# Last sums of weight conversions moved to GpSimd, two conversions moved out of the prologue, and the split middle products issued last

## The chip, the cores and the metric

The kernel runs on one core of a Trainium2 chip. The metric is device time in microseconds (us) of one execution. The names of the engines are those of the profile: PE is TensorE (matmuls; PEld its weight loads), DVE VectorE, ACT ScalarE, POOL GpSimd, SP the engine that here only issues DMAs. An engine works through its own instructions in the order in which they were issued; engines wait for each other by semaphores. DMAs are issued from the queues of SP, ACT and POOL.

## The reference

Two stages, one behind the other. First a global filter along the sequence: for each of 8 batches and 256 channels, a real Fourier transform over 3008 positions, a product with a complex filter, and the inverse transform. Then a feed-forward layer over all 24064 tokens.

```python
X = np.fft.rfft(x, axis=1)                    # x: (8, 3008, 256)
y = np.fft.irfft(X * (filt_r + 1j * filt_i)[None], n=3008, axis=1)
h = y.reshape(24064, 256) @ w_in              # (256, 2048)
out = (h - np.tanh(h)) @ w_out                # (2048, 256)
```

w_in and w_out come as 64-bit floats, the rest as 32-bit floats. All matmuls are in f32; a matmul stands in the trace as two records, one for each pass over the data.

## The kernel before

**The transform** is written with 3008 = 64 x 47, as matmuls with constant matrices, in three stages per batch. The *first* stage (`first`, product `pf`, line 294 for batches 1 and 2, 306 for the others) takes the 64-point part, four rows per step; its PSUM result is copied by ACT into the tile `a1` (line 296), of which there is one, and written to DRAM. The *middle* stage (`middle`, for batches 1 to 7) takes the 47-point part, the filter and the way back, in four steps `o` per batch. Each step has two matrix products, there and back, through `packed`: 24x24 matrices on 16 tiles of the PE array (four row groups `q`, four column groups `col`), each with 512 columns of data. In the last step, o=3, four of the 16 tiles hold special frequencies: there the 512 columns are split in two matmuls of 256 columns, one with the plain and one with the special matrix (line 358; all others are line 354). The *last* stage (`last`, product `pu`, line 534) gives the token block for the feed-forward layer.

**The feed-forward layer** runs in 48 groups (batch, part), each in four quarters `u` of the 2048 columns: 192 blocks, numbered U. One pass of the loop over U issues the up product of block U, the activation (`shrink`, on ACT lines 687 to 693, then DVE line 697) of block U-1 and the down product of block U-2. For the first group (U=0 to 3) these are plain products (`up_plain`, matmuls line 645, results copied by ACT or DVE in line 648; `down_plain`, line 800). From U=4 on they use a 2x2 block scheme with seven instead of eight products (`up`, line 575, `down`, line 745), for which sums of weight parts (`sums`, lines 223 and 226) and of data (`combine`, lines 555 to 558) are needed. `combine` runs on DVE while weights are still pending, and on POOL afterwards.

**The weights** are converted on the chip. `parts_of` cuts them into 16 jobs, here j0 to j15: j0 and j1 are quarter 0 of w_in (tile `wu`), j2 and j3 quarter 1, j4 and j5 quarter 2, j6 and j7 quarter 0 of w_out (tile `wd`), j8 and j9 quarter 3 of w_in, j10 to j15 the other quarters of w_out. A job is a generator, `converted`: a DMA of 512 KB into a raw buffer (line 169), a step on ACT (line 175), five on DVE (lines 177, 180, 183, 186 and 188) and a final sum of two halves into `wu` or `wd` (line 195; one instruction of 512 columns for w_in, two of 256 for w_out). The generator `weights` goes through a list of jobs, one step for each call of `next`. It issues the load of the job three further on when a job has been issued whole, and starts the next job's ACT step ahead of the current one's line 183. It also puts the calls of `sums(u)` behind certain jobs.

**Order of the work.** All of it is issued in the order of the Python program. The prologue (to line 1209) does batch 0's transform; its loop over seven slots `g` issues, for each, PE products (`across`, `there0`, `back0`), the filter (`filtered`, DVE lines 386 to 398, and on POOL the sum of line 395 for g below 5), and a few steps of the first five conversions (`convert`). At g=1 a row block `neg` is negated and written to `less`, and read back into the filter (line 489, on POOL's queue). At g=2 the raw loads of j5 and j6 are issued on POOL (line 1195). After the prologue's loop `convert(100)` issues what is left of j3 and j4; then come matmuls without use that keep PE busy (`warmer`), and the loop over U.

In the loop, the callbacks d, e, s and t that `up` and `up_plain` call set the order: d and e advance the down product, s the activation, e and the five calls t(0) to t(4) also advance the conversions (`converting`), t issues first-stage steps at the positions `due` (position 5u+k in the first group), middle-stage steps, and copies of the filter in DRAM (`filters_d`, lines 1250 and 1254, on POOL's queue). Four conversion steps are issued ahead of the loop, 14 in each of U=0 and 1, and 22 in each later block, until j15 and the sums of u=0 to 6 are done (103 steps, early in U=5).

In U=0, ACT copies all four up results to SBUF, in order; from U=1 on it copies the first and the third, DVE the second and the fourth.

Of the kernel before, what the change touches and what calls it, by code (L numbers as in the profile page):

```python
# [17 lines left out]
BATCH, SEQ, DM = 8, 3008, 256  # L18
# [9 lines left out]
NX = NH // XH  # L28
# [10 lines left out]
LEAD = 34  # L39
# [72 lines left out]
def kernel(  # L112
# [9 lines left out]
    nc = tc.nc  # L122
    V, G, ACT = nc.vector, nc.gpsimd, nc.scalar
# [41 lines left out]
    def converted(tiles, src, dsts, queue):  # L165

        n = src.shape[-1] * (src.shape[1] if len(src.shape) == 3 else 1)
        t = tiles("raw", I64, n)
        queue.dma_start(t if len(src.shape) == 2 else
                        t.rearrange("p (h n) -> p h n", h=src.shape[1]), src)  # L170
        yield
        words = t.bitcast(I32).rearrange("p (n w) -> p n w", w=2)
        lo, hi = words[:, :, 0].bitcast(U32), words[:, :, 1]
        top, low = tiles("top", I32, n), tiles("low", I32, n)
        ACT.activation(top.bitcast(F32), hi.bitcast(F32), AF.Copy, scale=2.0 ** -112)
        yield
        V.tensor_scalar(out=top.bitcast(F32), in0=top.bitcast(F32), scalar1=-MOST, scalar2=MOST,
                        op0=ALU.max, op1=ALU.min)
        yield
        V.tensor_scalar(out=top, in0=top, scalar1=5, scalar2=2,  # L180
                        op0=ALU.logical_shift_left, op1=ALU.logical_shift_right)
        yield
        V.scalar_tensor_tensor(out=top, in0=hi, scalar=-2 ** 30, in1=top,
                               op0=ALU.bitwise_and, op1=ALU.bitwise_or)
        yield
        V.tensor_scalar(out=low, in0=top, scalar1=-2 ** 23, scalar2=None, op0=ALU.bitwise_and)
        yield
        V.scalar_tensor_tensor(out=low.bitcast(F32), in0=lo, scalar=2.0 ** -52,
                               in1=low.bitcast(F32), op0=ALU.mult, op1=ALU.mult)
        for cols, dst in dsts:  # L190
            yield
            f, p = (v.bitcast(F32)[:, cols] for v in (top, low))
            if len(dst.shape) == 3:
                f, p = (v.rearrange("p (h n) -> p h n", h=dst.shape[1]) for v in (f, p))
            V.tensor_add(dst, f, p)
        yield

    def parts_of(quarters):
# [21 lines left out]
    def sums(u):  # L220

        w = (wu if u < 4 else wd)[:, :, 256 * (u % 4):256 * (u % 4) + 256]
        V.tensor_add(w[:, 4], w[:, 6], w[:, 3])
        yield
        for to, one_in, less in ((5, 4, 0), (2, 1, 5), (6, 0, 6)):
            V.tensor_sub(w[:, to], w[:, one_in], w[:, less])
            yield

    def begun(tiles, job, queue=nc.sync):
        j = converted(tiles, *job, queue)  # L230
        next(j)
        return j
# [112 lines left out]

    def packed(banks, o, weight, data):

        for q, bank in enumerate(banks):
            part = slice(PAD * q, PAD * q + NH)
            for col in range(4):  # L350
                to, at = bank[PAD * col:PAD * col + PAD], data(q, col)[part]
                plain, special = (wide[part, weight(q, col, last)] for last in (0, 1))
                if o < 3 or 3 != (col if weight is WAYS[0] else q):
                    nc.tensor.matmul(to.rearrange("p n c -> p (n c)"), plain, at,  # L354
                                     start=True, stop=True)
                    continue
                for n, way in enumerate((plain, special)):
                    nc.tensor.matmul(to[:, n], way, at[:, n * DM:n * DM + DM],  # L358
                                     start=True, stop=True)

    def forth(g, at, z):

# [584 lines left out]
    with tc.tile_pool(name="tr", bufs=2) as tr, tc.manual_schedule():  # L947
# [16 lines left out]
        with tc.tile_pool(name="pro", bufs=1) as pro, \  # L964
# [106 lines left out]
            jobs = parts_of((0, 1, 2, 4, 3, 5, 6, 7))  # L1071
# [38 lines left out]
            began.append(begun(tiles0, jobs[2], queue=G))  # L1110
            G.dma_start(mats[:, 3 * KM:6 * KM], mats_d[:, 3 * KM:6 * KM])
            fts[1] = filters_of(1)
            began += [begun(tiles0, job, queue=G) for job in jobs[3:5]]
            G.dma_start(mats[0:KH, 6 * KM:], mats_d[0:KH, 6 * KM:])
            turning = turned_rows(tr.tile([128, 2, DM], F32, tag="e1", bufs=2, name="neg")[0:NH, 0])
            next(turning)

            early = weights(tiles0, jobs[:5], G, began, 5)
            next(early)

            def convert(n):
# [44 lines left out]
            for g in range(last_g + 1):  # L1166
# [25 lines left out]
                if g == 1:  # L1192
                    next(turning)
                if g == 2:
                    ahead = [begun(tiles1, job, queue=G) for job in jobs[5:7]]
            rest(0, SG * (last_g - 1), [nc.sync])
            way_back()
            rest(SG * (last_g - 1), NA - SG * (last_g - 1), [nc.sync])
# [2 lines left out]
            fs = first(2, z2, [(1, c) for c in range(2, NX)])  # L1201
            next(fs)
            convert(100)
            late = weights(tiles1, jobs[5:], G, ahead, 3,
                           after={6: (0,), 8: (1,), 10: (2, 3, 4, 5, 6)})
            next(late)
            for _ in ones_1:
                pass
# [2 lines left out]
        with tc.tile_pool(name="dn", bufs=2) as dn, \  # L1211
# [60 lines left out]
                                 start=True, stop=True)  # L1272
            for _ in range(4):
                next(late)
            due = [4 + (LEAD - 4) * k / (NX + 4) for k in range(NX + 4)]
            plan = []
            kinds = {(2, 0): "there", (1, 3): "back"}
            kinds.update({at: "filter" for at in FILTERED})
# [2 lines left out]
            for U in range(total + 2):  # L1281
# [25 lines left out]
                def converting(n):  # L1307

                    for _ in range(n):
                        if next(late, pending) is pending:  # L1310
                            pending.clear()
# [5 lines left out]
                def e():  # L1317

                    next(dw, None)
                    converting(3 if U > 1 else 1)  # L1320

                def s():

# [85 lines left out]
```

## Time and profile before

| | us |
|---|---|
| median of 3 runs | 2591.28 |
| lowest and highest run | 2586.17, 2592.92 |
| profiled execution | 2591.19 |
| its span, first to last instruction | 2589.4 |
| PE busy in the span | 2561.4 |
| granted clock, mean | 0.998 |

The profile has one row for each group of instructions, and a timeline with one row for each run of like instructions: start, duration, engine, line, operation, written tile <- read tiles, shapes and count. In brackets stands how long the engine had been idle before it and what ended the wait. Of an engine's 99% nothing follows for one stretch: the prologue, the first blocks and the long steady part are read one by one. Times in the timeline count from the span's start; the first up product of the loop starts at 88.18 us.

### The profile page before, as it was taken

To read this page: it belongs to the slowest core of one execution; us is meant where nothing else is said; L and a number is where in the kernel's file an instruction comes from. 1 tells how busy PE (TensorE), PEld (TensorE's weight loads), DVE (VectorE), ACT (ScalarE), POOL (GpSimd) and SP (SyncE) were. 2 spreads that over 40 slices of the span, in tenths; PEclk is the share of its full clock that TensorE was granted. 3 is DMA by queue.
4 is the path that set the end of the run, shared out by engine and by line. 5 is a ranking of instruction groups with operands and counts; after the bars stand their busy time and mean duration, and the time that the engine had idled before them with its cause. 6 is when DMAs were issued, how large, how long until landed. Compare 5 with 4: busy or idle time off the path is not lost.

```text
span 2589.4 us, 43444 instructions
## 1 busy us (share of the span) xinstructions
PE 2561.4 (99%) x16596; PEld 2180.3 (84%) x16596; DVE 1818.5 (70%) x2234; ACT 1662.5 (64%) x2482; POOL 1466.0 (57%) x1126
## 2 busy tenths in 40 slices
PE   8999999999999999999999999999999999999998
PEld 6668888888898888988888888888889888898887
DVE  6788776877567775778657876588766877555555
ACT  4566666666666666666666666666666666666665
POOL 4356665665556655665646565466655766545552
PEclk9999999999999999999999999999999999999999
DMA  7873215441433324333243432444231321110110
GB/s 219 259 194 103 64 33 120 110 102 44 95 80 100 89 56 92 84 90 92 49 101 80 101 79 50 94 96 104 65 68 45 93 66 41 35 33 18 25 22 18
DMA packets 345334, 214.32 MB, mean 83 GB/s; under 512 B 245337, under 2 KB 316535, under 8 KB 341469
## 3 DMA queue, kind: packets, MB, share of 16 engines
q1 hardware_dynamic: 321551, 170.82, 28.7%
q10 hardware_dynamic: 12142, 23.60, 3.0%
q0 software_dynamic: 11424, 17.03, 2.4%
q8 instruction: 133, 2.18, 0.4%
q14 instruction: 84, 0.69, 0.1%
HBM read 130.72 MB, written 83.39 MB: 83 GB/s over the span
## 4 chain that ended last, share of the span: by engine, by line
PE 95%; DMA 2%; DVE 1%; ACT 1%; issue 1%; POOL 0%; ACTq 0%; DVEq 0%; POOLq 0%
PE o L745 43%; PE x L575 25%; PE z L575 12%; PE y L575 6%; PE pm L354 2%; PE pu L534 2%; DMA ct<-a 2%; PE pf L306 1%; PE pm L358 1%; PE warm L996 0%; PE pf L986 0%; DMA neg<-in_filt_i_dram 0%; PE o L800 0%; PE pe L1047 0%; PE pf L294 0%
## 5 line engine op out<-in xcount | busy, mean ns | idle before, releaser
L745 PE MATMUL o<-t,wd 128*128 128x256 f32 (+1 forms) x3008 | 762.1, 376 | 0.0
L555 POOL TENSOR_TENSOR t<-h 128x512 f32<-128x512 f32 (+1 forms) x186 | 305.2, 1641 | 747.8 <-DVE h L697 709.3
L697 DVE TENSOR_TENSOR h<-h,y 128x1024 f32<-128x1024 f32 (+1 forms) x384 | 575.8, 1499 | 169.3 <-ACT y L693 165.7
L745 PEld LDWEIGHTS o<-t,wd 128*128 128x128 f32 x3008 | 569.2, 190 | 82.5 <-POOL o L773 15.1
L575 PE MATMUL x<-tu,wu 128*128 128x256 f32 (+1 forms) x2256 | 579.0, 379 | 0.0
L745 PE MATMUL o<-h,wd 128*128 128x256 f32 (+1 forms) x2256 | 572.8, 376 | 1.8 <-DVE h L697 1.8
L581 ACT COPY s<-x 128x512 f32<-128x512 f32 (+1 forms) x188 | 108.8, 579 | 603.0 <-PE x L575 554.1
L745 PEld LDWEIGHTS o<-h,wd 128*128 128x128 f32 x2256 | 426.0, 190 | 71.4 <-issue 20.5
L575 PEld LDWEIGHTS x<-tu,wu 128*128 128x128 f32 x2256 | 421.0, 190 | 66.8 <-issue 12.9
L690 ACT ACTIVATE y<-y 128x1024 f32<-128x1024 f32 (+1 forms) x384 | 399.3, 1040 | 12.1
L693 ACT ACTIVATE y<-y 128x1024 f32<-128x1024 f32 (+1 forms) x384 | 399.8, 1041 | 4.6
L687 ACT ACTIVATE y<-h 128x1024 f32<-128x1024 f32 (+1 forms) x384 | 400.3, 1042 | 3.5 <-DVE h L623 1.7
L556 POOL TENSOR_TENSOR t<-h,t 128x512 f32<-128x512 f32 (+1 forms) x186 | 306.2, 1646 | 14.6
L557 POOL TENSOR_TENSOR t<-h 128x512 f32<-128x512 f32 (+1 forms) x186 | 288.3, 1550 | 0.0
L558 POOL TENSOR_TENSOR t<-h,t 128x512 f32<-128x512 f32 (+1 forms) x186 | 287.4, 1545 | 0.0
L581 ACT COPY u<-x 128x512 f32<-128x512 f32 (+1 forms) x376 | 213.8, 569 | 56.2 <-PE x L575 53.5
L623 DVE COPY h<-x 128x512 f32<-128x512 f32 (+1 forms) x188 | 128.0, 681 | 139.9 <-PE x L575 139.6
L575 PE MATMUL x<-ut,wu 128*128 128x256 f32 (+1 forms) x752 | 190.1, 375 | 1.4 <-DVE h L623 1.4
L575 PE MATMUL z<-ut,wu 128*128 128x256 f32 (+1 forms) x752 | 190.1, 375 | 0.2 <-DVE h L615 0.2
L575 PE MATMUL y<-ut,wu 128*128 128x256 f32 (+1 forms) x752 | 190.1, 375 | 0.1
L575 PE MATMUL z<-tu,wu 128*128 128x256 f32 (+1 forms) x752 | 190.0, 375 | 0.0
L598 DVE TENSOR_TENSOR h<-y,s 128x512 f32<-128x512 f32 (+1 forms) x188 | 126.6, 674 | 68.6 <-PE y L575 61.7
(195 smaller groups left out, 2777.3 us busy)
## 6 DMA issues: line engine op xcount, KB each, us to landing
ft<-filt SPq DMA_DIRECT2D x28, 1024.0 KB
ct<-nn SPq DMA_DIRECT2D x56, 512.0 KB
e<-ct SPq DMA_DIRECT2D x47, 512.0 KB
a<-ct SPq DMA_DIRECT2D x112, 192.0 KB
out_dram<-ot SPq DMA_DIRECT2D x1248, 16.0 KB
x_sb<-in_x_dram SPq DMA_DIRECT2D x74, 256.0 KB
ct<-a ACTq DMA_DIRECT2D x62, 256.0 KB
gt<-g_pairs SPq DMA_DIRECT2D x42, 128.0 KB
```

The costliest lines, as they stand in the source:

```text
L555: by.tensor_sub(t[0], b[0][1], b[0][0])
L556: by.tensor_sub(t[1], b[1][1], t[0])
L557: by.tensor_sub(t[2], b[1][1], b[0][1])
L558: by.tensor_sub(t[3], b[1][0], t[1])
L575: nc.tensor.matmul(bank[:, k], wu[:, q - 1, (2 * u + k) * 128:(2 * u + k + 1) * 128], rhs[q - 1], start=(first and k == 0), stop=True, ski ...
L581: ACT.copy(t, X)
L623: V.tensor_copy(h[:, 2, :, 0:w], X)
L687: ACT.activation(y[k], ht[k], AF.Arctan, scale=TURN)
L690: ACT.activation(y[k], y[k], AF.Tanh, scale=BEND)
L693: ACT.activation(y[k], y[k], AF.Square, scale=SCALE, accum_out=y_sums[:, 2 * U + k // 2:2 * U + k // 2 + 1])
L697: V.tensor_mul(ht[k], ht[k], y[k])
L745: nc.tensor.matmul(product(q), wd[:, q - 1, (2 * u + k) * 128: (2 * u + k + 1) * 128], rhs[q - 1][:, k], start=(u == 0 and k == 0 and q == ...
```

## The change

Six edits, one diff. (1) The final sum of every conversion (line 195) is issued on POOL instead of DVE. (2) Only j0 to j2 are converted in the prologue. The raw loads of j3 and j4 are no longer issued at its start; they take the place that those of j5 and j6 had at g=2, and the list in the loop begins with j3. It now has 13 jobs and 115 steps. (3) In U=0 and 1 `e` advances the conversions by three steps, as in the later blocks, so that each block has 22. (4) The first-stage steps of the loop are due from position 7 instead of 4 (7, 9.7, 12.4 and so on up to 31.3, instead of 4, 7, 10 up to 31). (5) The sums of weights for u=4, 5 and 6 (parts of wd) run on POOL. (6) In `packed`, the four special matmuls of a split product are collected and issued behind all 16 plain ones, instead of each right behind the plain one of its tile.

```diff
@@ converted
-            V.tensor_add(dst, f, p)
+            G.tensor_add(dst, f, p)
@@ sums
-        V.tensor_add(w[:, 4], w[:, 6], w[:, 3])
+        by = G if 4 <= u < 7 else V
+        by.tensor_add(w[:, 4], w[:, 6], w[:, 3])
         yield
         for to, one_in, less in ((5, 4, 0), (2, 1, 5), (6, 0, 6)):
-            V.tensor_sub(w[:, to], w[:, one_in], w[:, less])
+            by.tensor_sub(w[:, to], w[:, one_in], w[:, less])
             yield
@@ packed
+        late = []
         for q, bank in enumerate(banks):
             part = slice(PAD * q, PAD * q + NH)
             for col in range(4):
                 to, at = bank[PAD * col:PAD * col + PAD], data(q, col)[part]
                 plain, special = (wide[part, weight(q, col, last)] for last in (0, 1))
-                if o < 3 or 3 != (col if weight is WAYS[0] else q):
-                    nc.tensor.matmul(to.rearrange("p n c -> p (n c)"), plain, at,
-                                     start=True, stop=True)
-                    continue
-                for n, way in enumerate((plain, special)):
-                    nc.tensor.matmul(to[:, n], way, at[:, n * DM:n * DM + DM],
-                                     start=True, stop=True)
+                if o == 3 and 3 == (col if weight is WAYS[0] else q):
+                    late.append((to[:, 1], special, at[:, DM:2 * DM]))
+                    to, at = to[:, 0], at[:, 0:DM]
+                else:
+                    to = to.rearrange("p n c -> p (n c)")
+                nc.tensor.matmul(to, plain, at, start=True, stop=True)
+        for to, special, at in late:
+            nc.tensor.matmul(to, special, at, start=True, stop=True)
@@ the prologue
-            began += [begun(tiles0, job, queue=G) for job in jobs[3:5]]
...
-            early = weights(tiles0, jobs[:5], G, began, 5)
+            early = weights(tiles0, jobs[:3], G, began, 3)
...
-                    ahead = [begun(tiles1, job, queue=G) for job in jobs[5:7]]
+                    ahead = [begun(tiles1, job, queue=G) for job in jobs[3:5]]
...
-            late = weights(tiles1, jobs[5:], G, ahead, 3,
-                           after={6: (0,), 8: (1,), 10: (2, 3, 4, 5, 6)})
+            late = weights(tiles1, jobs[3:], G, ahead, 3,
+                           after={8: (0,), 10: (1,), 12: (2, 3, 4, 5, 6)})
@@ the loop over U
-            due = [4 + (LEAD - 4) * k / (NX + 4) for k in range(NX + 4)]
+            due = [7 + (LEAD - 7) * k / (NX + 4) for k in range(NX + 4)]
...
-                    converting(3 if U > 1 else 1)
+                    converting(3)
```

## Prediction

> **What bounds the kernel.** The page comes first, then a table of busy time by stretch, then the timelines of single engines.
>
> ```profile
> span 2589.4 us, 43444 instructions
> PE 2561.4 (99%) x16596; PEld 2180.3 (84%) x16596; DVE 1818.5 (70%) x2234; ACT 1662.5 (64%) x2482; POOL 1466.0 (57%) x1126
> ```
>
> ```profile
> 0.00:85.00 85.00, 72.64 (x387) 60.97 (x387) 56.99 (x92) 32.75 (x55) 33.78 (x52) 0.98 0.75 206
> 85.00:135.00 50.00, 47.00 (x261) 28.43 (x262) 40.17 (x75) 30.36 (x51) 22.62 (x30) 0.97 1.01 301
> 135.00:340.00 205.00, 202.73 (x1263) 163.57 (x1263) 160.45 (x212) 133.92 (x201) 126.12 (x92) 1.00 0.44 111
> 340.00:2560.00 2220.00, 2220.00 (x14602) 1912.14 (x14601) 1546.62 (x1834) 1455.93 (x2163) 1282.09 (x951) 1.00 0.31 71
> ```
>
> The columns of the second view are the stretch, its length, the busy time of PE, PEld, DVE, ACT and POOL, the granted clock, the DMA share and GB/s. From 340 to 2560 us PE is busy in all 2220.00 us at clock 1.00: there only what shortens PE's own work counts, and DVE or POOL work is free as long as it stays hidden. Before 340 PE idles 12.4 us in the prologue, 3.0 us in the first blocks and 2.3 us after. All of the change but one part lies in those first 160 us, and the DMA engines are full from 85 to 135 us (share 1.01). I sum against the profiled execution: span 2589.4 us, 2591.2 us with what lies around it; the median shown, 2591.3 us, is the same number.
>
> **Part 1, split middle products last.** This is the part inside the PE-bound stretch.
>
> ```profile
> 222.10 1.89 PE L745 MATMUL o<-t,wd 128*128 128x256 f32 x8
> 223.92 1.14 PE L354 MATMUL pm<-xy,mats_sb 24*32 24x512 f32 x32
> 224.99 0.48 PE L575 MATMUL x<-tu,wu 128*128 128x256 f32 x1
> ```
>
> ```profile
> 381.43 0.69 PE L354 MATMUL pm<-xy,mats_sb 24*32 24x512 f32 x12
> 381.96 0.95 PE L358 MATMUL pm<-xy,mats_sb 24*32 24x256 f32 x7
> ```
>
> ```profile
> 382.50 1.07 PE L358 MATMUL pm<-xy,mats_sb 24*32 24x256 f32 x7
> 383.50 0.48 PE L575 MATMUL x<-tu,wu 128*128 128x256 f32 x1
> ```
>
> ```profile
> L358 PE MATMUL pm<-a,mats_sb x112: 374/374/398, 333.9 to 2148.4; 24*32 24x256 f32 x112
> L358 PE MATMUL pm<-xy,mats_sb x112: 371/374/398, 381.5 to 2196.8; 24*32 24x256 f32 x112
> ```
>
> Each matmul stands twice in the records (two passes). A product that isn't split (16 tiles, 32 records) runs from 223.92 to 224.99: 1.07 us, its tiles side by side. A split one runs from 381.43 to 383.50: 2.07 us. 224 records of L358 are 14 products with four tiles, two halves and two passes. Inside the split one, the first 16 matmuls start at once; then single records, and from 382.50 (1.07 us in) the last seven, strung over 1.0 us because a plain product is still among them, with its special behind it on the same tile. So a 17th matmul doesn't go fully ahead until the first of the 16 is done. In the new order the 16 plain ones fill that room exactly and the four specials, each on a tile of its own, come 17th to 20th. The first finishes its start at 1.07, the other three run side by side behind it: 2 passes of 0.22 us (the eight from 222.10 to 223.92 took 1.82), 0.02 to get going and 0.09 to empty the array as in the unsplit product: 1.07 + 0.02 + 0.44 + 0.09 = 1.62 us. That saves 0.45 x 14 = **6.3 us**. Bounds: nothing, or the whole difference to an unsplit product, 1.00 x 14 = 14.0. I take 6.3, since the row that it hangs on is a split product's own. The Trainium skill (TensorEngine Tiling (Array Packing), Key Properties) says that tiles operate independently and matmuls on different tiles run in parallel; by that the specials would start when their tile's short plain half ends, and the saving would be 14.0. The trace agrees for the 16 but not for the 17th.
>
> **Part 2, the prologue.** DVE loses three sums (0.69 us each) and the first steps of j3; POOL gets the sums and loses two raw loads.
>
> ```profile
> 33.83 1.26 POOL L395 TENSOR_TENSOR nn<-nn,xy 120x512 f32<-120x512 f32 x1
> 33.96 1.42 DVE L180 TENSOR_SCALAR top<-top 128x512 int32<-128x512 int32 x1
> 48.04 0.68 POOL L489 DMA_DIRECT2D filt<-less  x1 [5.39 <-DMA less<-neg]
> 48.74 1.28 POOL L395 TENSOR_TENSOR nn<-nn,xy 120x512 f32<-120x512 f32 x1
> 50.05 0.59 ACT L372 COPY xy<-pa 120x512 f32<-120x512 f32 x1 [1.64 <-POOL nn L395]
> 51.23 0.49 DVE L177 TENSOR_SCALAR top<-top 128x512 f32<-128x512 f32 x1 [2.83 <-ACT top L175]
> 86.97 0.69 DVE L541 TENSOR_TENSOR ut<-pu,odd 128x512 f32<-128x512 f32 x1 [6.06 <-ACT odd L538]
> ```
>
> The relief of DVE is mostly not on the path: at 51.23 DVE has waited 2.83 us for ACT, ACT for POOL's L395, and L395 stood behind the load of the turned filter rows (L489), which waited 5.39 us for a write. POOL works in order, and j1's sum is issued behind L489 and ahead of L395. It adds one POOL sum (taken at 1.28 us, L395's) to exactly this chain; all later prologue work follows it. Against it stand tenths: the two raw loads and DVE's sums no longer stand ahead of that write (up to 0.5 us, or nothing, since j0's sum now stands ahead of the L395 at 33.83), and L395 no longer meets j3's first step. Sum: **+1.0 us**, from -1.5 (clock 0.98 over the 85 us is 1.7 us of PE work lost at half clock; if the waits that bring it shift apart, most of it goes) to +1.8. The two conversions that leave the prologue's end save nothing: DVE idles 6.06 us there. Their raw loads take the places that those of j5 and j6 have now, in POOL's queue behind that L395, so as many are on the way as before.
>
> The 1.42 us of L180 beside POOL's sum, against 0.43 alone (below), is the price of sums on POOL: the next conversion's first step stands still until the sum is done. The Trainium skill (SBUF — State Buffer, Who interferes with whom) has this as an exclusive lock between DVE and GpSimd. The trace agrees in this row; by it each moved sum saves DVE 0.69 and costs it 0.99.
>
> **Part 3, the first blocks (U=0 to 2).** Here lies the step on which most hangs.
>
> ```profile
> 88.04 0.42 DVE L177 TENSOR_SCALAR xy<-xy 128x512 f32<-128x512 f32 x1
> 88.49 0.43 DVE L180 TENSOR_SCALAR xy<-xy 128x512 int32<-128x512 int32 x1
> ...
> 90.14 0.69 DVE L188 SCALAR_TENSOR_TENSOR xy<-ft,xy 128x512 f32<-128x512 uint32 x1
> ```
>
> ```profile
> 85.35 0.74 POOL L169 DMA_DIRECT2D a<-in_moe_w_out_dram  x1 [0.37 <-issue]
> 86.09 0.74 POOL L169 DMA_DIRECT2D a<-in_moe_w_in_dram  x1
> ```
>
> ```profile
> DMA to landing us min/median/max: 6.0/9.7/10.7
> ```
>
> ```profile
> 93.00 0.53 ACT L648 COPY h<-o 128x448 f32<-128x448 f32 x1 [0.97 <-PE o L645]
> 93.42 0.69 ACT L175 ACTIVATE xy<-a 128x512 f32<-128x512 f32 x1
> 97.03 1.07 ACT L296 COPY a<-pf 128x512 f32<-128x512 f32 x2 [2.00 <-DMA ct<-a]
> ...
> 99.56 0.95 ACT L687 ACTIVATE y<-h 128x896 f32<-128x896 f32 x1
> ```
>
> ```profile
> 100.53 1.89 PE L294 MATMUL pf<-x_sb,f 128*128 128x256 f32 x8
> 102.26 1.67 PE L645 MATMUL o<-ut,wu 128*128 128x448 f32 x4
> 103.77 1.67 PE L645 MATMUL x<-ut,wu 128*128 128x448 f32 x4
> 108.43 3.21 PE L294 MATMUL pf<-x_sb,f 128*128 128x256 f32 x8 [3.00 <-DMA x_sb<-in_x_dram]
> 111.43 0.95 PE L800 MATMUL o<-h,wd 128*128 128x448 f32 x1
> ```
>
> (The landing times are those of all transfers into tile a from 80 to 140 us.) The load of a raw block is issued on POOL as soon as the block three before it has been emitted. So far nothing of a conversion ran on POOL: at 85.35 and 86.09 two loads went out back to back. Now the sum of j3 stands in POOL's queue ahead of j6's load, j4's ahead of j7's, j5's ahead of j8's. And 22 instead of 14 steps per block in U=0 and 1 put ACT's first step of j6 (step 17) between the third and fourth copy of U=0, that of j7 behind the fourth, that of j8 after two activations of U=1.
>
> Worked on the old clock: j3's DVE steps run from 88.04 to 90.83, its sum to 92.3; then j6's load is issued and lands 6.2 us later at 98.5 (near the row's least: fewer loads are under way at once than when it took 9.7). ACT stands from 94 to 98.5, does the step and the fourth copy to 99.7. j4's steps wait for the lock until 92.3 and end at 95.0, its sum at 96.3, j7's load lands at 102.5, ACT copies U=1's first product by 103.7. j5's sum ends at 100.0, j8 lands at 106.2; step, two activations, a copy and another activation to 110.3, half a first-stage copy (L296) to 110.9. PE meanwhile has its blocks of 1.50 us (102.26 to 103.77) and the now later first-stage step (1.73): U=1 ends at 101.9, the first product of U=2 waits until 103.7 and ends at 105.2, and the next first-stage step needs its PSUM banks back from that copy: PE idles from 105.2 to 110.9. Then, as after the 3.00 us idle now, the step goes at half clock (3.0 instead of 1.73), so the down product (L800) starts at 113.9, with one first-stage step (1.73) still owed: worth 115.6 against 111.43. Cost **+4.2 us**; the old wait of 3.00 us for x_sb and its half clock are counted in. If ACT never stood for a raw block, U=2's first product would end at 103.4 and the down product be worth 106.9: -4.5. If the loads took 9.7 us: +7.6. I take 4.2, its landing being nearest to the lesser load on the queues.
>
> **Part 4, U=4 and 5.**
>
> ```profile
> 149.46 1.13 PE L294 MATMUL pf<-x_sb,f 128*128 128x256 f32 x4 [0.49 <-DVE h L598]
> 155.57 1.13 PE L575 MATMUL z<-ut,wu 128*128 128x256 f32 x4 [0.24 <-DVE h L615]
> 158.09 1.13 PE L575 MATMUL x<-ut,wu 128*128 128x256 f32 x4 [1.39 <-DVE h L623]
> ```
>
> PE waits 2.1 us for DVE, which does conversions and sums there. With more steps done earlier and the wd sums of u=4 to 6 on POOL, DVE sheds most of j15's steps (2.8 us, as the run from 88.04 to 90.83) and those sums in U=4, more than the waits are long: **-2.1 us**, with +2 as the other end, if late raw blocks hold ACT here instead. POOL's twelve sums are hidden as long as POOL idles ahead of its first combine. Later raw blocks, U=3 included, I take as hidden: ACT is busy 30.36 of the 50 us from 85 to 135.
>
> **Sum.** 1.0 + 4.2 - 2.1 - 6.3 = -3.2 us: 2591.2 - 3.2 = **2588.0 us**, with 2583 to 2594 as this case's own range. A measurement of this kernel can tell about 0.3%, 7.8 us, from no change.
>
> **The rivals.**
> Raw blocks hold nobody (the loads land before ACT comes to them, or another wait hides it): part 3 gives -4.5, the total 2591.2 - 11.9 = 2579.3. For it: ACT's slack now, and that no row shows ACT waiting for a raw block; against it: the order of POOL's queue. Chance 0.20.
> The specials overlap wholly (the skill's rule above): part 1 gives 14.0, the total 2580.3. For it: the side-by-side start of the 16; against it: the gap up to 382.50. Chance 0.17.
> The reordering does nothing on PE, the specials being as long in a row of their own: 2594.3. Against it: the unsplit product's 1.07. Chance 0.10.
> Slower: POOL becomes the bound. Its sums queue behind the issue of loads and filter copies, raw blocks land after 9.7 us, and ACT stands for them in U=2 and U=3 as well. Part 3 is 7.6 instead of 4.2, and its 4.2 comes twice more: +3.4 + 8.4 - 3.2 = +8.6, 2599.8 us. It decides from the point where ACT stands for a raw block in U=3 too. For it: POOL in order and DMA full; against it: POOL idles over half of 85 to 135 (22.62 us busy). Chance 0.13.
>
> **How the numbers follow.** The forecast has 0.40. Faster by over 0.3%: the first two rivals without their edges, 0.36; slower: the last, 0.13; within: the rest, 0.51. The range 2577 to 2599 leaves out most of the slow rival and the two fast ones together.
>
> **What would show it.** Split products of 1.6 us instead of 2.07. A POOL sum between L489 and the L395 after it, and the first block later than 85 us. ACT idle ahead of L175 in U=0 and 1 with the DMA of raw blocks as its end, and PE idle ahead of the second pf. No PE waits near 150 to 158 us. The prediction is wrong if the raw loads aren't behind the sums in POOL's queue, if ACT has something else ahead of them, or if the 17th matmul waits for something other than room.

## The result, and the profile after

| | before | after |
|---|---|---|
| median, us | 2585.98 (20 runs) | 2591.86 (20 runs) |
| lowest to highest, us | 2583.53 to 2592.92 | 2589.00 to 2598.75 |
| profiled execution, us | 2591.19 | 2594.66 |

The ratio after to before is 1.0019, with a 95% interval of 1.0013 to 1.0026: slower by about 0.2%, within the 0.3% that was named as no change. The forecast had 2588.0 and a gain of 3.2 us. With 20 runs in place of 3, the kernel before stands at 2586.0, so the execution that the forecast was summed against lies 5.2 us above the median. The profiled execution after lies 2.8 us above its own.

The page of the changed kernel, and its stretches (columns as in the prediction). Most line numbers are one to six higher than before: the plain down product, L800 before, is L803 here.

```profile
span 2592.8 us, 43449 instructions
PE 2559.0 (99%) x16596; PEld 2177.9 (84%) x16596; DVE 1814.0 (70%) x2198; ACT 1661.3 (64%) x2482; POOL 1498.7 (58%) x1162
```

```profile
0.00:85.00 85.00, 74.53 (x451) 63.00 (x452) 48.99 (x77) 31.41 (x53) 37.42 (x54) 0.96 0.73 200
85.00:135.00 50.00, 42.21 (x120) 24.13 (x121) 46.43 (x70) 28.09 (x46) 30.68 (x37) 0.93 0.82 250
135.00:340.00 205.00, 200.39 (x1271) 161.73 (x1270) 153.48 (x187) 132.51 (x200) 141.79 (x114) 0.99 0.48 121
340.00:2560.00 2220.00, 2220.00 (x14658) 1911.33 (x14657) 1549.15 (x1842) 1457.04 (x2166) 1286.51 (x955) 1.00 0.31 72
```

From 340 us on PE is busy throughout, as before. The loss lies in the second and third rows: PE is busy 42.21 of 50 us instead of 47.00, at clock 0.93 instead of 0.97, and then 200.39 of 205 instead of 202.73. In the second row DVE, without the sums but with two conversions more in the loop, went from 40.17 to 46.43 us busy.

**Split products.** The timeline of PE around the first one, whose partner before took 2.07 us:

```profile
389.66 1.11 PE L360 MATMUL pm<-xy,mats_sb 24*32 24x512 f32 x32
390.30 1.08 PE L362 MATMUL pm<-xy,mats_sb 24*32 24x256 f32 x8
391.31 1.13 PE L578 MATMUL x<-tu,wu 128*128 128x256 f32 x4
```

From 389.66 to 391.31 are 1.65 us. That is 0.41 less for each of 14 products, 5.8 us in all; the forecast had 1.62 us and 6.3.

**Prologue.** The timeline of POOL:

```profile
46.16 0.69 POOL L492 DMA_DIRECT2D filt<-less  x1 [3.56 <-DMA less<-neg]
46.86 1.28 POOL L195 TENSOR_TENSOR wu<-top,low 128x512 f32<-128x512 f32 x1
48.09 1.27 POOL L398 TENSOR_TENSOR nn<-nn,xy 120x512 f32<-120x512 f32 x1
```

The sum of j1 stands where the forecast put it, and takes the 1.28 us. But the read back was over 1.88 us earlier (46.16 against 48.04), so the filter's sum still comes 0.65 earlier, and the loop's first up product at 86.95 us instead of 88.18. One execution can't show this gain, though. Nine profiles with the prologue of before (the kernel before twice, and e3, e6, e7, e9, e12, e14 and e16 below) start the loop between 85.96 and 88.68 us, five with edits 1 and 2 (the changed kernel, e2, e8, e10 and e17) between 86.40 and 88.69; both means are 87.65.

**First blocks.** ACT and then PE, in U=0 to 2:

```profile
95.80 0.68 ACT L175 ACTIVATE xy<-a 128x512 f32<-128x512 f32 x1 [3.53 <-DMA a<-in_moe_w_out_dram]
...
98.84 0.69 ACT L175 ACTIVATE xy<-ft 128x512 f32<-128x512 f32 x1 [1.94 <-DMA ft<-in_moe_w_out_dram]
...
103.55 0.70 ACT L175 ACTIVATE xy<-ft 128x512 f32<-128x512 f32 x1 [1.76 <-DMA ft<-in_moe_w_in_dram]
```

```profile
107.81 3.45 PE L295 MATMUL pf<-x_sb,f 128*128 128x256 f32 x8 [5.36 <-ACT a L297]
111.10 1.67 PE L803 MATMUL o<-h,wd 128*128 128x448 f32 x4
```

ACT stands three times for raw blocks, as forecast, and PE waits 5.36 us (forecast 5.7) ahead of the second first-stage step, which then goes at half clock. The down product starts at 111.10, 0.33 us earlier than before, but the loop began 1.23 earlier, and a first-stage step (1.73) is still owed: the stretch cost 2.6 us against the profiled execution of before, where part 3 had 4.2.

**U=3 and U=4.** Here the forecast had a gain of 2.1 us. POOL, then PE and ACT:

```profile
120.90 0.55 POOL L1235 MEMSET zero<- 128x512 f32 x1
...
122.87 2.17 POOL L1243 DMA_DIRECT2D filt<-zero  x4
125.03 0.74 POOL L1252 DMA_DIRECT2D filt<-in_filt_r_dram  x1
125.78 2.27 POOL L195 TENSOR_TENSOR wd<-xy 128x256 f32<-128x256 f32 x2
```

```profile
128.11 1.86 PE L803 MATMUL o<-h,wd 128*128 128x448 f32 x2 [2.34 <-POOL wd L195]
...
141.56 1.97 PE L295 MATMUL pf<-x_sb,f 128*128 128x256 f32 x8 [1.62 <-issue]
...
150.39 1.13 PE L578 MATMUL y<-ut,wu 128*128 128x256 f32 x4 [2.99 <-ACT a L297]
```

```profile
148.72 0.66 ACT L175 ACTIVATE xy<-ft 128x512 f32<-128x512 f32 x1 [7.64 <-DMA ft<-in_moe_w_out_dram]
```

The sum of j11 stands behind the filter copies in POOL's queue, and PE's down product waits for it. Later ACT waits 7.64 us for the raw block of j15, whose load POOL issued at 136.83 us (125.84 before), and PE waits for the copy behind that. The waits for DVE, which the forecast wanted gone, are gone. After 83 us PE's idle stretches sum to 12.5 us (5.4 before), and the clock is half in three places behind them instead of one.

What this cost can be read at the second middle product, which stood at 223.92 us before; in both kernels the same work lies ahead of it:

```profile
232.56 1.14 PE L360 MATMUL pm<-xy,mats_sb 24*32 24x512 f32 x32
```

From U=2's first down product to here are 121.46 us, 119.73 without the first-stage step that was still owed; before, 112.49. So this stretch cost 7.2 us. Of these, 4.8 are PE's waits (2.34, 1.62 and 2.99 us, for 0.49, 0.24 and 1.39 before). With the prologue and the first blocks the changed kernel is 8.6 us late at this product.

### The profile page after: what moved, and what is told of

Read it like the earlier page. It is cut to its first block, busy times and chain, and to the rows that moved or that the text cites. A ratio compares the mean times of both kernels' runs of the same rounds, so it can differ in the third digit from the quotient of the medians.

```text
span 2592.8 us, 43449 instructions
## 1 busy us (share of the span) xinstructions
PE 2559.0 (99%) x16596; PEld 2177.9 (84%) x16596; DVE 1814.0 (70%) x2198; ACT 1661.3 (64%) x2482; POOL 1498.7 (58%) x1162
## 4 chain that ended last, share of the span: by engine, by line
PE 94%; POOL 2%; DMA 2%; issue 1%; DVE 1%; ACT 0%; ACTq 0%; SPq 0%; POOLq 0%; DVEq 0%
PE o L748 43%; PE x L578 25%; PE z L578 12%; PE y L578 6%; PE pm L360 2%; PE pu L537 2%; PE pf L307 1%; PE o L803 1%; DMA x<-in_x_dram 0%; DMA ft<-in_moe_w_out_dram 0%; DMA raw<-in_moe_w_in_dram 0%; PE pm L362 0%; PE pf L295 0%; POOL wd L195 0%; POOL wu L195 0%
## 5 line engine op out<-in xcount | busy, mean ns | idle before, releaser
L601 DVE TENSOR_TENSOR h<-y,s 128x512 f32<-128x512 f32 (+1 forms) x188 | 126.6, 673 | 69.5 <-PE y L578 62.9
```

## The experiments

Each time is the median difference to the kernel before in runs on the same chip; the ratio has its 95% interval. Three theories stood at the start. **Q**, the queue: sums on POOL delay the raw loads and are delayed by the filter copies. **W**, the work: more conversions, and more of their steps for each block, stand between the copies that PE needs. **L**, the lock: DVE stands still beside POOL's sums.

**e1, the conversions' sums back on DVE.**

```diff
-            G.tensor_add(dst, f, p)
+            V.tensor_add(dst, f, p)
```

> The changed kernel with one edit undone: the last sums of all conversions are on DVE again. Theory Q (queue): the 10 us lost between the loop's start and 175 us come from the sums in POOL's queue, ahead of the raw loads and behind the filter copies. Then PE's idle time after the loop's start falls from 12.3 us (5.4, 2.3, 1.6 and 3.0) to under 4, ACT no longer stands for raw blocks, and the kernel is 5 to 9 us faster than the one before. Rival W (work): the loss comes from two more conversions in the loop at 22 steps per block, whoever adds; then the idle time stays near 12 and the kernel is 3 to 6 us slower than before.

Measured +4.4 us (1.0016, 1.0007 to 1.0025): within 1.5 us of the changed kernel, and PE idles 11.2 us after the loop's start. By itself that speaks for W and against Q. But PE's waits are in other places, and in U=4 DVE is now late, as PE's timeline says:

```profile
150.66 1.13 PE L295 MATMUL pf<-x_sb,f 128*128 128x256 f32 x4 [2.01 <-DVE h L601]
...
159.55 2.08 PE L578 MATMUL z<-ut,wu 128*128 128x256 f32 x4 [3.02 <-DVE h L618]
```

**e2, raw loads four jobs ahead instead of three, in the changed kernel.**

```diff
-            late = weights(tiles1, jobs[3:], G, ahead, 3,
+            late = weights(tiles1, jobs[3:], G, ahead, 4,
```

> The changed kernel with raw loads issued four jobs ahead instead of three; sums stay on POOL. Theory Q: the loads of j6 and later go out one job earlier, ACT's waits for raw blocks in U=0 and 1 vanish, PE idles under 7 us after the loop's start (the wait for a sum behind filter copies stays), and the kernel is between 5 us faster and 1 us slower than the one before. Rival L (lock): sums on POOL hold DVE's next step, 1.37 instead of 0.43 us, and that is what delays the blocks; then nothing changes, 4 to 7 us slower than before.

Measured +3.6 us (1.0011, 1.0002 to 1.0020), between Q's range and L's. The raw blocks of j6 and j7 now come in time, and ACT stands all the same; its timeline:

```profile
96.45 0.69 ACT L175 ACTIVATE xy<-a 128x512 f32<-128x512 f32 x1 [2.13 <-POOL wu L195]
...
100.10 0.68 ACT L175 ACTIVATE xy<-ft 128x512 f32<-128x512 f32 x1 [2.55 <-POOL wu L195]
```

It waits for the tile that POOL's sum of an earlier job still reads. These sums follow each other every 3.66 us (91.39, 95.05, 98.71), and in the kernel before, with the sums on DVE, a conversion took 3.4 to 3.5 us (the first steps of three in a row start at 88.04, 91.48 and 94.99). The forecast's raw load was the last of ACT's waits, and another stood right under it: the pace of the conversions, which the sums on POOL don't raise.

**e3, the split order alone**, in the kernel before (edit 6).

> The kernel before with the split products reordered and nothing else. All theories: 14 products at 1.65 instead of 2.07 us, 5.8 us faster than before, and no difference ahead of the first split product.

Measured -5.6 us (0.9973, 0.9962 to 0.9984). Part 1 is confirmed by itself.

**e4, all final sums on POOL alone**, in the kernel before (edit 1).

> The kernel before with the last sums of all conversions on POOL and nothing else: five conversions in the prologue, 14 steps in U=0 and 1. Theory Q: loads stand behind sums here too, PE idles at least 4 us longer after the loop's start and the kernel is 3 to 8 us slower than before. Rival W: no change, within 1.5 us. Rival L: up to 2 us slower, with DVE late and no ACT wait for raw blocks.

Measured +7.3 us (1.0026, 1.0017 to 1.0035): Q's range, but PE idles only 0.5 us longer after the loop's start than in the profiled execution of before, not 4. Its longest wait is for a sum behind filter copies:

```profile
128.25 1.86 PE L800 MATMUL o<-h,wd 128*128 128x448 f32 x2 [4.03 <-POOL wd L195]
```

Alone, the edit costs at least as much as the whole change; undone (e1), it gives back almost nothing. So the next four take the other edits apart.

**e5, edits 2, 3 and 6**; **e6, edits 4 and 6**; **e7, edits 5 and 6**, each in the kernel before; **e8, the changed kernel with first-stage steps due from 4** (edit 4 undone).

> The kernel before with the split middle products issued last, and with edits 2 and 3: three conversions in the prologue, 13 in the loop, 22 steps in every block; all sums stay on DVE and the first-stage steps are due from 4. With the split order alone the kernel was 5.6 us below the one before. Theory W (what the two conversions in the loop bring is the cost, wherever their sums run: more raw transfers and more steps between the copies of ACT and DVE that PE needs): this kernel is 0 to 5 us above the one before, 6 to 11 above the split order alone. Rival D (the later first-stage steps of edit 4 are the cost): 4 to 8 us below the one before. Rival P (sums of down weights on POOL, edit 5, behind which raw loads and filter copies queue): 4 to 8 us below the one before.

> The kernel before with the split middle products issued last, and with edit 4 alone: first-stage steps due from position 7 instead of 4. Theory W: the place of these steps is worth little by itself, 4 to 7 us below the kernel before. Rival D: 3 us below to 2 above. Rival P: 4 to 7 us below.

> The kernel before with the split middle products issued last, and with edit 5 alone: the sums of weights of u=4, 5 and 6 on POOL. My forecast took 2.1 us of waits away by this and by earlier conversions. If these sums are hidden on POOL and DVE's waits in U=4 go: 6 to 8 us below the kernel before. Rival P (the sums stand in POOL's queue ahead of its first combine, and hold DVE at the lock): 3 us below to 3 above. Theory W: 4 to 8 below.

> The changed kernel with edit 4 undone: first-stage steps due from position 4 again. Theory W: within 1.5 us of the changed kernel, so 3 to 6 us above the one before. Rival D: 4 to 8 us below the changed kernel, so 4 below to 1 above the one before. If the later steps help, as ACT has more room for raw blocks ahead of them: 6 to 10 us above the one before.

Measured: e5 -2.2 us (0.9993, 0.9984 to 1.0002), e6 -5.7 (0.9977, 0.9968 to 0.9987), e7 +2.3 (1.0010, 1.0001 to 1.0019), e8 +4.3 (1.0014, 1.0005 to 1.0023). Edit 4 costs nothing by itself and little in the changed kernel, so D falls. Edits 2 and 3 cost 3.4 us over e3, less than W said and more than its rivals. Edit 5, which the forecast had down as a relief, costs 7.9: P is right in size. Its place shows on DVE, in the pair of final sums of j14, in e7 and then in e3:

```profile
143.49 2.96 DVE L195 TENSOR_TENSOR wd<-xy 128x256 f32<-128x256 f32 x2
```

```profile
146.18 0.76 DVE L195 TENSOR_TENSOR wd<-xy 128x256 f32<-128x256 f32 x2
```

and in what POOL does meanwhile, and PE waits for behind it, in e7:

```profile
144.75 1.41 POOL L227 TENSOR_TENSOR wd<-wd 128x256 f32<-128x256 f32 x2
```

```profile
148.83 1.13 PE L295 MATMUL pf<-x_sb,f 128*128 128x256 f32 x4 [4.06 <-DVE h L601]
```

POOL has nothing to wait for and does the sums of wd at once, from 141.03 us on, beside DVE's last two conversions; the pair takes 2.96 instead of 0.76 us, and L601, DVE's sum of two products of `up` (L598 before), stands behind it in DVE's order.

**e9, the same sums held back** until DVE has done its own; **e10, the changed kernel with edit 5 undone**; **e11 and e12, the filter copies on SP's queue**, with edit 1 and without. F is what of Q the filter copies make.

```diff
...
+        if u == 4:
+            G.tensor_copy(held, wu[:, 6, 1023:1024])
...
```

```diff
-                G.dma_start(dram(filt_d,
+                nc.sync.dma_start(dram(filt_d,
...
```

> The kernel before with the split order and with edit 5 (sums of down weights on POOL, alone 2.3 us above the kernel before, where the split order by itself is 5.6 below it), plus one POOL copy of a single element of wu, ahead of the first of these sums, that waits for DVE's last sum of u=3. So POOL's twelve sums no longer run beside DVE's last conversions. Theory L (beside POOL's sums each DVE step takes up to twice as long, and PE waits for the activation behind them): the loss goes, 3 to 8 us below the kernel before. Theory F (what costs is the time that these sums take in POOL's queue, ahead of filter copies): it stays or grows, since the copies now wait longer, 0 to 6 us above the kernel before.

> The changed kernel with edit 5 undone: the sums of weights of u=4, 5 and 6 on DVE again, the conversions' final sums still on POOL. If the losses of edits 1 and 5 add up (+7.3 and +8 alone): 5 to 9 us below the changed kernel, so 4 below to 1 above the one before. If they are the same loss, taken once (in the changed kernel DVE's conversions end so late that POOL's sums of down weights come behind them): within 2 us of the changed kernel, so 3 to 7 above the one before.

> The kernel before with edit 1 alone (all final sums on POOL, by itself 7.3 us above the kernel before), and with the copies of the filter in DRAM issued from SP's queue instead of POOL's. To be read against the next kernel, which has the copies on SP without the sums. Theory F (in the block U=3 the sum of a down weight stands behind some 8 us of filter copies in POOL's queue, and PE's down product waits for it): the sums now cost 0 to 2.5 us. Theory L (DVE stands at the lock beside each sum): they still cost 5 to 8.

> The kernel before with nothing changed but the queue of the filter copies: SP's instead of POOL's. The control for the kernel with the sums. In the kernel before nothing waits for POOL in these blocks, so I expect it within 2 us of the kernel before, or up to 5 above if the loads of x on SP come later behind the copies.

Measured: e9 -4.6 us (0.9978, 0.9969 to 0.9987), e10 +5.5 (1.0018, 1.0009 to 1.0027), e11 +38.4 and e12 +31.8 (1.0142, 1.0126 to 1.0157, and 1.0121, 1.0105 to 1.0137). In e9 the same twelve sums run on POOL and the loss of e7 is gone. DVE's pair of sums and POOL's wait there:

```profile
142.91 0.76 DVE L196 TENSOR_TENSOR wd<-xy 128x256 f32<-128x256 f32 x2
```

```profile
152.36 0.18 POOL L226 COPY held<-wu 128x1 f32<-128x1 f32 x1 [11.25 <-DVE wu L230]
```

From U=2's first down product to the second middle product e7 takes 120.0 us, e9 112.8 and e3 112.3. So it isn't POOL's time, or the filter copies behind these sums (they now come 11 us later), but that they run beside DVE's conversions: L is shown for edit 5 without edit 1. The Trainium skill (SBUF — State Buffer, Who interferes with whom) says that a DVE instruction with two inputs in SBUF contends with a GpSimd one that reads SBUF, and that the shared ports are an exclusive lock; 2.96 against 0.76 us for DVE's pair, with and without POOL's sums beside it, agrees. e10 shows that in the changed kernel edits 1 and 5 cost once, not twice. There, with the final sums on POOL, DVE's last conversion ends at 152.85 us, and POOL's sums of wd come behind it:

```profile
156.37 1.25 POOL L224 TENSOR_TENSOR wd<-wd 128x256 f32<-128x256 f32 x1
```

e11 and e12 tell little. They differ by 6.6 us, as L says for the sums (5 to 8), but on SP the copies hold the loads of the middle stage, as PE's row in e12 says, and that drowns what was to be seen:

```profile
190.05 5.76 PE L354 MATMUL pm<-a,mats_sb 24*32 24x512 f32 x32 [21.76 <-DMA a<-ct]
```

**e13, edit 1 with the six zero copies issued one by one**; **e14 and e15, edit 1 for j10 to j15 and for j0 to j9 alone**; **e16, edits 3 and 6** (in e16 the sums of weights of u=6 are, by the count of steps, issued ahead of the plain down product of U=2 that still reads those weights, so that its output is wrong; the work has the same size).

```diff
                             zeros[0:30])
+                yield
...
                             zeros[0:2, 0:DM])
+                yield
...
-                yield
+                    yield
```

```diff
-            V.tensor_add(dst, f, p)
+            by.tensor_add(dst, f, p)
...
+                jobs.append((src, dsts, G if k > 4 else V))
```

> The kernel before with edit 1 alone (7.3 us above the kernel before), and with the six zero copies at the start of the filter copies issued one for each call instead of all in one, so that no more than two of them stand ahead of a sum at a time. Theory F (PE's wait of 4.0 us for a down weight comes from the run of copies ahead of its sum): 1 to 4 us above the kernel before. Theory L (the lock): 5 to 9 above.

> The kernel before with the final sums of j10 to j15 alone on POOL, those that meet the filter copies in its queue. Theory F: 5 to 8 us above the kernel before, the whole cost of edit 1. Theory L: the six late sums cost their share of the eleven in the loop, 2 to 5 above.

> The kernel before with the final sums of j0 to j9 alone on POOL; no filter copy stands ahead of these. Theory F: within 2 us of the kernel before. Theory L: 2 to 5 above. My forecast's theory for the first blocks (raw loads behind these sums, and ACT waiting for them) says 2 to 6 above too, and shows it in waits of ACT for raw loads.

> The kernel before with the split order and with edit 3 alone: 22 conversion steps in U=0 and 1 as in the later blocks, five conversions in the prologue as before. The split order alone is 5.6 us below the kernel before, with edits 2 and 3 2 below. If the steps by themselves hurt (ACT comes to raw blocks before they have landed, and PE waits for copies behind them): 3 below to 1 above. If the two conversions more are the cost: 4 to 8 below, as conversions that end earlier leave DVE free in U=4.

Measured: e13 +5.4 us (1.0018, 1.0009 to 1.0027), e14 +4.0 (1.0014, 1.0005 to 1.0023), e15 +7.0 (1.0024, 1.0015 to 1.0034), e16 -0.4 (0.9995, 0.9986 to 1.0004). F as the whole cause falls: the early sums, which meet no filter copy, cost as much as all. But so does L as it was put, since e15 is above its 2 to 5. In e15 another queue shows, in the prologue, POOL and then DVE:

```profile
84.29 0.18 POOL L1200 COPY there_yet<-e 128x1 f32<-128x1 f32 x1 [13.04 <-DMA f<-f_both]
84.43 1.26 POOL L195 TENSOR_TENSOR wu<-top,low 128x512 f32<-128x512 f32 x1
```

```profile
85.73 0.43 DVE L186 TENSOR_SCALAR low<-top 128x512 int32<-128x512 int32 x1 [6.48 <-POOL wu L195]
```

The sum of j3 stands behind a copy that waits 13.04 us for a load, and j4 stands behind it. In the four kernels with this queue (e4, e11, e13, e15) the loop starts at 88.68 to 91.39 us, against 85.96 to 88.68 with the prologue of before. With three conversions in the prologue (edit 2) these two sums come later, in the loop. e16 has the dearest edit outside POOL: 22 steps in U=0 and 1 cost 5.2 us over e3, and edit 2 on top of it gains 1.8 (e5), which is within the uncertainty. In e5, and in e1, which has edit 2 with all sums on DVE as well, the loop starts at 86.07 and 86.13 us. ACT's first waits in e16 have the same form as in the changed kernel, with all sums on DVE:

```profile
93.22 0.68 ACT L175 ACTIVATE xy<-a 128x512 f32<-128x512 f32 x1 [1.18 <-DMA a<-in_moe_w_out_dram]
95.91 0.69 ACT L175 ACTIVATE xy<-a 128x512 f32<-128x512 f32 x1 [1.59 <-DVE xy L180]
...
99.25 0.68 ACT L175 ACTIVATE xy<-ft 128x512 f32<-128x512 f32 x1 [1.26 <-DMA ft<-in_moe_w_in_dram]
```

**e17, the changed kernel with 18 steps in U=0 and 1**; **e18, the kernel before once more**, with a profile. S is W's part in the steps.

```diff
-                    converting(3)
+                    converting(3 if U > 1 else 2)
```

> The changed kernel with 18 instead of 22 conversion steps in U=0 and 1 (before: 14). Theory S (in order, ACT must take the first step of the next conversion ahead of copies that PE waits for, and conversions follow each other only every 3.7 us; more steps for each block make ACT stand): 1 to 4 us below the changed kernel, so 1 to 4 above the one before, and PE's wait ahead of the second pf shorter than 5.4 us. If the steps cost nothing beside sums on POOL: within 1 us of the changed kernel, 4 to 6 above the one before.

> The kernel before, unchanged, with another profile. If PE's wait of 3.0 us for x_sb and the half clock behind it belong to some executions alone, this one has a span of 2582 to 2586 us without them; if they are always there, the span differs in other places, and they stand here as well.

Measured: e17 +3.7 us (1.0015, 1.0006 to 1.0024), 2.2 below the changed kernel, which is within the uncertainty and between the two expectations. PE's waits in it:

```profile
107.45 3.48 PE L295 MATMUL pf<-x_sb,f 128*128 128x256 f32 x8 [3.48 <-ACT a L297]
130.54 1.86 PE L803 MATMUL o<-h,wd 128*128 128x448 f32 x2 [5.06 <-POOL wd L195]
```

The first wait is shorter, as S said (3.48 against 5.36 us), but the wait for j11's sum in U=3 grew from 2.34 to 5.06 us. In this one execution, what is taken from one is paid at the other. e18 came to 2590.76 us, again with the wait:

```profile
107.75 2.60 PE L294 MATMUL pf<-x_sb,f 128*128 128x256 f32 x8 [3.13 <-DMA x_sb<-in_x_dram]
```

Both profiled executions of the kernel before have it, and both are slower than its median (2588.03 us in e18's runs). Of the other profiles with 14 steps in U=0 and 1, PE has no wait there in e6, e7, e9, e12 and e14, about 1 us in e4, e13 and e15, and 2.3 and 3.2 in e11 and e3. In all eight with 18 or 22 steps (the changed kernel, e1, e2, e5, e8, e10, e16, e17) it waits 2.3 us or more. From the loop's first up product to the first down product, with three first-stage steps, the kernel before (twice), e3 and e16 take 22.7 to 23.5 us, and e6, e7, e9, e12 and e14, without the wait, 18.8. That the quicker executions of the kernel before also lack it is likely by this, but was not seen.

## Why the prediction was wrong

The account of the change, from the differences between runs: split order -5.6 (e3), edit 3 +5.2 (e16 less e3), edit 2 -1.8 (e5 less e16), edit 4 nothing (e6 less e3), edits 1 and 5 together +8.1 (the changed kernel less e5): +5.9 us, the difference of the medians, because the last term was taken as the rest. What checks it is that e10 and e1, each with one of edits 1 and 5, are 7.7 and 6.6 above e5. Each difference between two kernels is uncertain by some 3 us. The forecast's terms can be set against the profiled executions; in brackets stands the range over the five profiles with edits 1 and 2 (the changed kernel, e2, e8, e10, e17), all against the one execution of before.

| stretch | forecast, us | measured, us |
|---|---|---|
| part 2, to the loop's first up product | +1.0 | -1.2 (-1.8 to +0.5) |
| part 3, to U=2's first down product | +4.2 | +2.6 (+0.4 to +2.6) |
| part 4, to the second middle product | -2.1 | +7.2 (+2.9 to +7.2) |
| part 1, 14 split products | -6.3 | -5.8 |
| sum | -3.2 | +2.8 |

The spans of the two profiled executions differ by 3.4 us; the 0.6 that the sum lacks lies behind the second middle product. The medians differ by 5.9, since the execution before stands higher in its spread (5.2 us above the median) than the one after (2.8).

**Part 1 held in its size**: 5.6 to 5.8 us for 6.3. Neither the rival of whole overlap (14.0) nor that of no effect came. The order inside wasn't as written: by the records the specials begin 0.64 us into the product, not at 1.07, so that 1.65 us came out near 1.62 by some luck.

**Part 2 had the right cost and too small a relief.** The added sum stands where it was put, and takes the 1.28 us; the wait ahead of it fell from 5.39 to 3.56 us, more than the sum takes. The text had that as "up to 0.5 us, or nothing". Over all profiles nothing is left of it: the loop starts at a mean of 87.65 us with edits 1 and 2 as without, and some 1.5 earlier with edit 2 and all sums on DVE (e1, e5).

**Part 3 had the right mechanism, and probably a gain in it that most executions don't give.** ACT's waits for raw blocks, PE's 5.4 us and the half clock came as written, and against the profiled execution the stretch cost 2.6 us for 4.2. But "the old wait of 3.00 us for x_sb and its half clock are counted in": they are worth 4.4 us (some 23.2 us with them, 18.8 without), in an execution that was 5.2 above the median. Against 18.8 us the stretch costs the changed kernel 7.1. The mechanism's base was off too: e2 shows that the landing of the loads, on which the 4.2 hung, is not the only thing that ACT stands for.

**Part 4 is the step that failed**, with the sentence "Later raw blocks, U=3 included, I take as hidden": -2.1 us forecast, +7.2 measured (at least +2.9 in the other four profiles). The waits for DVE went, as written, but others came in their place: 2.34 us for j11's sum, which stands behind filter copies in POOL's queue, and 2.99 us for a copy of ACT behind j15's raw block. The text knew the second as its other end, "+2 as the other end, if late raw blocks hold ACT here instead", and chose against it; ACT busy for 30.36 of 50 us was no proof that it has time at the right place. "POOL's twelve sums are hidden" failed in another way. Without edit 1 they run beside DVE's last conversions and hold them: +7.9 us (e7), about +1 when they are held back (e9). In the changed kernel they come behind these conversions, and undoing edit 5 gives next to nothing (e10). Part 2 had quoted the row for the lock, L180 at 1.42 instead of 0.43 us, and used it for the conversions' sums only.

**The slow rival** named U=3, and POOL's queue with loads and filter copies as cause, and its waits came. As a difference, the measured +5.9 us is nearer to its +8.6 than to the forecast's -3.2. That 2591.9 us is nearer to 2588.0 than to its 2599.8 is luck: both start from an execution that was 5.2 us slow.

**What stays open**: how the cost of edit 1 divides between the pace of the conversions, held by the lock (3.66 against 3.4 to 3.5 us), and the places in POOL's queue, in the prologue and in U=3. A version of edit 1 with neither wasn't tried. e13 to e15 say that no one place carries it. Nor do the profiles show the 5 us between e16 and e3 (spans 2583.6 and 2583.0). Both have PE's wait ahead of a first-stage step; e3's profiled execution is the slowest of its runs, e16's is an ordinary one. So it may be that 22 steps make a common thing of a wait that 14 steps have now and then, but that isn't shown.

The changed kernel keeps one edit worth having: e3, e6 and e9 are all some 5 us below the kernel before and some 11 below the changed one.

## What to carry to other kernels

An operation moved from one engine to another frees the first only if the first isn't held while the second works: look in the trace for the same instruction with and without the other engine beside it, and apply what it shows to every moved operation, not to the first one alone. New work in a queue delays all that stands behind it: ask what that is at every place, the later ones too. When undoing one edit gives nothing back, undo two: here either of two edits brought about the whole loss, and each hid the other. Ahead of a sum of a few microseconds, know where the profiled execution stands in the spread of the times, and don't count as a gain a wait that may be missing in most executions.

## What the runs showed of the hardware

- With all 16 tiles of PE in use, four more matmuls on four of them begin, by the records, 0.64 us into the product and overlap with the plain ones; the whole takes 1.65 us, and 2.07 with plain and special interleaved (1.07 without specials).
- Beside POOL's additions two DVE additions took 2.96 us instead of 0.76, and POOL's own addition of 128x256 up to 1.19 us instead of 0.73 (e7).
- The filter copies into DRAM, for which PE waits nowhere on POOL's queue in the kernel before, cost 31.8 us on SP's, where loads stand behind them (e12).
- Behind PE's waits the granted clock fell: 0.66, 0.72 and 0.72 in the three stretches of the changed kernel in this view:

```profile
107.00:112.00 5.00, 4.19 (x11) 3.21 (x12) 4.61 (x7) 4.25 (x9) 1.94 (x2) 0.66 0.68 231
126.00:132.00 6.00, 3.89 (x6) 1.91 (x7) 5.86 (x8) 2.89 (x4) 6.00 (x7) 0.72 1.04 347
150.00:156.00 6.00, 5.61 (x15) 3.74 (x16) 5.83 (x10) 4.15 (x7) 4.37 (x6) 0.72 0.86 216
```

A clock of 0.66 over 5 us, or 0.72 over 6, is 3.4 us at half clock, and 1.7 us of PE's work lost behind a wait of 2.3 to 5.4 us. The Trainium skill (TensorE: Matmul & The Clock Gate, What's actually happening) has a free-running window of about 3.4 us by which the clock is halved; the length agrees. The length of a wait of about 2 us doesn't tell whether it comes: 1.95 us in e8 brought it (0.66 from 127 to 132 us), 2.19 us in e6 and 2.33 us in e5 and e8 did not.
